# A gated mix of linear and softmax attention on one core: pieces of the output weights rest while the kernel changes halves, and the gate's blocks begin later

## The chip, the cores and the metric

The kernel runs on one core of a Trainium2 chip. The metric is the device time of one execution in microseconds (us), as the median of several runs. Beside the timed runs there is one execution under the hardware profiler; all rows below are from it.

## The reference

```python
def reference(A_x, A_wqkv, A_wo, B_x, B_wqkv, B_wo, gate_w):   # x: 1 x 2048 x 1024, 32 heads of 32
    ...
    x = A_x
    g = _sigmoid((x * gate_w).sum(-1, keepdims=True))
    a = _A_ref(x, A_wqkv, A_wo)      # linear attention: phi(q) (phi(k)^T v) / (phi(q) sum phi(k)), then @ A_wo
    b = _B_ref(x, B_wqkv, B_wo)      # softmax attention over 2048 x 2048 scores per head, then @ B_wo
    return g * a + (1 - g) * b
```

All tensors are float32. The kernel splits each operand into a high part in the reduced format float32r and a low rest, and takes three products (high·high, high·low, low·high) in place of one.

## The kernel before

All instructions of a core's engines are put into their queues in program order, written out by a Python program. Each engine works its queue strictly in order and waits on semaphores for the others. SP issues most transfers, POOL (GpSimd) the rest.

**The first 422 us are a hand-written order.** It has these stages:

- The first half of the tokens is loaded and split, and the first 512 columns of the softmax side's v are computed in eight passes (`v_pass`, one for each block of 128 rows of weights). The weights' splits are stored in DRAM (`wv`).
- `quads(0, ...)` and a last `quad(0, QUADS - 1, ...)`: eight quads, of seven products each, that give the softmax side's q and k for the first half of the tokens by a scheme that needs seven block products in place of eight. A product is 4 × 3 matmuls of 128×512. VectorE (DVE) adds the products (L469 to L486), ScalarE (ACT) and DVE split the results (L294, L295), SP stores them (`qk<-mid`). The same two engines prepare the next quad's weights (`quad_weights`, L428 to L443) from tiles that SP has loaded.
- The products go to six PSUM banks in turn (`turns`, `NQB`): a product has to wait until the adds have read the product six places earlier. The second product of a quad waits so for the adds that end with L478 of the quad before.
- The change of halves: beside the last quad, `change()` loads the stored v weights again (`big<-wv`) and splits the first blocks of the second half of the tokens; then come eight more `v_pass`es, with the splitting of the other blocks (`split_x`, `sides`, `split_sides`), the loading of the first quads' weights, and the copies of v from the banks (`v_out`, L358). The first product of the next quad needs a bank that `v_out` has read.
- `quads(1, ...)` and a last quad: the same for the second half of the tokens.

**The pieces of the output weights** are made beside this. `wo_parts` (L494) is a generator that prepares `b_wo` for the output's seven products: 28 pieces, each with a small copy on ACT (L511) that paces it, a small copy on POOL (L512), a cast and a subtraction on POOL (L513, L514), two stores of 256 KB (L516), on POOL's queue, and, by kind, another POOL subtraction (L524, L531, L537) and a load of 256 KB (L502). It is advanced once at each `next(side, None)` of a quad, seven times a quad, and in the kernel before also twice in each of the eight passes: 49 + 7 + 16 + 49 + 7 = 128 calls. How often a piece comes is set by `PIECE_STEP`:

```python
def wait():
    at[0] += PIECE_STEP
    while next(turn) + 1 < at[0]:
        yield
```

**From 422 us on a planner sets the order.** It keeps a model time for each engine (`T`) and picks the next instruction for PE from four streams: the linear side (`linear`), which begins with the second 512 columns of v ("the last half of v", 16 tiles), the maxima of the scores (L1234, L1239), the heads (L1376, L1379, L1526), and the output. The tiles of the linear side read the split tokens in halves of 256 KB each for high and low (`load_half`; `xh<-xs` and `big<-xs`): three buffers, and a half is loaded into the buffer that has just been used.

**The gate's blocks** (`gate_step`, L553) lie in the last half of v: 32 blocks of the tokens are loaded by SP (`mid<-in_xT`, `zrep<-in_xT`) into four buffers in turn, scaled on ACT (L571), added on POOL (L577) and summed on PE (L585). The first block is issued when PE's model time, counted from the start of the last half of v, is at `GATE_FROM`, and each next one `GATE_STEP` later. A block's load waits on SP's queue until POOL's add has freed its buffer, and all later transfers of SP wait behind it.

Of the kernel before, what the change touches and what calls it, by code (L numbers as in the profile page):

```python
# [38 lines left out]
WARM = 8  # L39
NE = 3  # L40
AHEAD_X = 3
PIECE_STEP = 4.1
GATE_STEP, GATE_FROM = 2.5, 8.0
LATE = 1.0
MANUAL = {ET.PE, ET.DVE, ET.Activation, ET.SP, ET.Pool}
NMID = 13
# [3 lines left out]
def kernel(  # L50
# [34 lines left out]
    def f32r(ap):  # L85
        return ap.bitcast(F32R)
# [62 lines left out]
    def three(ps, stat, mov, kt, late=False, n=None):  # L149

        (sh, sl), (mh_, ml_) = stat, mov
        last = kt == (n or NK) - 1
        yield nc.tensor.matmul(ps, sh, mh_, start=(kt == 0), stop=False)  # L153
        if late:
            yield nc.tensor.matmul(ps, sl, mh_, start=False, stop=False)
        yield nc.tensor.matmul(ps, sh, ml_, start=False, stop=(late and last))  # L156
        if not late:
            yield nc.tensor.matmul(ps, sl, mh_, start=False, stop=last)  # L158
# [8 lines left out]
    def dma(to, of):  # L167

        T["sp"] = max(T["sp"], T["pe"]) + DMA_ISSUE
        nc.sync.dma_start(to, of)  # L170
# [122 lines left out]
    def split(hi, lo, src, eng):  # L293
        nc.scalar.copy(hi, src)  # L294
        eng.tensor_sub(lo, src, f32(hi))  # L295
# [21 lines left out]
    QUADS = 2 * NK // 2  # L317
    assert NK == 8 and NPAIR == 2

    def ring_w(n, p):  # L320

        b, half = RINGW[n % len(RINGW)]
        return big[b][:, (2 * half + p) * C:(2 * half + p + 1) * C]
# [4 lines left out]
    def quad_ring(J, f, s):  # L328
        return v_ring(J, NK) + f * NP + s
# [4 lines left out]
    def xpiece(J, name, p, i):  # L334
        return side_x(J, name, p)[:, i * C:(i + 1) * C]
# [32 lines left out]
    def split_x(raws, J, jj, k, c0=0, c1=C):  # L368
        name = xname(jj, k % 2)
        split(*(xpiece(J, name, p, k // 2)[:, c0:c1] for p in range(2)), raws[jj + 2 * (k % 2)][:, c0:c1], nc.vector)  # L370

    def sides(raws, i):

        r11, r12, r21, r22 = raws
        nc.vector.tensor_sub(r11, r12, r11)
        nc.vector.tensor_sub(r12, r22, r12)
        nc.vector.tensor_sub(r22, r22, r11)
        nc.vector.tensor_sub(t4_raw[i], r21, r22)
# [29 lines left out]
    def quad_cols(f):  # L408
        return f % 2, 2 * (f // 2)
# [37 lines left out]
    def quad(J, f, side):  # L447

        sec, g = quad_cols(f)

        def product(s):
            ps = bank[next(turns) % NQB]
            n = quad_ring(J, f, s)
            for i in range(KH):
                sl = slice(i * P, (i + 1) * P)
                stat = [ring_w(n, p)[:, sl] for p in range(2)]
                for _ in three(ps, stat, [xpiece(J, PRODUCTS[s], p, i) for p in range(2)], i, n=KH):
                    pass
            return ps

        def store(i, jj, src, hi):
            split(f32r(hi), f32r(src), src, nc.vector)
            j = 2 * J + jj
            for p, part in enumerate((hi, src)):
                dma(qk_d[sec][p][g + i][:, j * C:(j + 1) * C], part)

        nc.scalar.copy(P1, product(0))
        next(side, None)
        nc.vector.tensor_add(C11, product(1), P1)  # L469
        store(0, 0, C11, H11)  # L470
        next(side, None)
        p3 = product(2)
        next(side, None)
        p5 = product(3)
        next(side, None)
        nc.vector.tensor_add(U2, product(4), P1)
        nc.vector.tensor_add(W2, p5, U2)
        nc.vector.tensor_add(P1, p3, W2)  # L478
        store(0, 1, P1, H12)
        next(side, None)  # L480
        p7 = product(5)
        nc.vector.tensor_add(W2, p7, W2)
        nc.vector.tensor_add(U2, p7, U2)
        store(1, 1, W2, H22)
        next(side, None)
        nc.vector.tensor_add(U2, product(6), U2)  # L486
        store(1, 0, U2, H21)
        next(side, None)
# [5 lines left out]
    def wo_parts():  # L494

        z0, z1 = halves(zrep)
        hi_w, lo_w = (big[15][:, i * C:(i + 1) * C] for i in (2, 3))
        at, turn, tokens = [1.0], count(), count()

        def load(z, m, i, **add):  # L500
            if i < KH:
                nc.gpsimd.dma_start(z, wo_piece(m, i), **add)  # L502
# [6 lines that stand above are left out]
        def part(m, i, z):  # L509
            n = next(tokens) % (C // DH)  # L510
            nc.scalar.copy(dn[0][:, n:n + 1], eps)  # L511
            nc.gpsimd.tensor_copy(dn[1][:, n:n + 1], dn[0][:, n:n + 1])  # L512
            nc.gpsimd.tensor_copy(hi_w, z)  # L513
            nc.gpsimd.tensor_sub(lo_w, z, f32(hi_w))  # L514
            for p, src in enumerate((hi_w, lo_w)):
                nc.gpsimd.dma_start(wo_d[m][p][:, i * C:(i + 1) * C], f32(src))  # L516

        yield
        load(z1, "W11", 0)
        load(z0, "W21", 0)  # L520
        yield from wait()
        for i in range(KH):
            part("W11", i, z1)
            nc.gpsimd.tensor_sub(z1, z1, z0)  # L524
            load(z0, "W22", i, accum_op=ALU.add)
            yield from wait()
            part("S3", i, z1)
            load(z1, "W11", i)
            yield from wait()
            part("S1", i, z0)  # L530
            nc.gpsimd.tensor_sub(z0, z0, z1)  # L531
            load(z1, "W12", i)
            yield from wait()
            part("S2", i, z0)
            yield from wait()
            part("W12", i, z1)
            nc.gpsimd.tensor_sub(z1, z1, z0)  # L537
            load(z0, "W22", i)
            yield from wait()
            part("S4", i, z1)  # L540
            load(z1, "W11", i + 1)
            yield from wait()
            part("W22", i, z0)
            load(z0, "W21", i + 1)
            yield from wait()

    parts = wo_parts()
# [52 lines left out]
    def beside(*streams):  # L600

        streams = list(streams)
        while True:
            for s in list(streams):
                next(s, None)
            yield
# [30 lines left out]
    def load_wv_again(ks):  # L637
        for k in ks:
            for p in range(2):
                dma(f32(ring_w(v_ring(1, k), p)), wv_d[k][:, p * C:(p + 1) * C])  # L640
# [9 lines left out]
    def load_pair(raws, J, i):  # L650
        for k in (2 * i, 2 * i + 1):
            for jj in range(2):
                load_x(raws, J, jj, k)
# [52 lines left out]
    def change():  # L706

        load_wv_again(range(NK - 2))
        split_x(raw_x1[0], 1, 0, 0)
        yield  # L710
        load_wv_again([NK - 2])
        split_x(raw_x1[0], 1, 1, 0)
        yield
        load_wv_again([NK - 1])
        split_x(raw_x1[0], 1, 0, 1)
        yield
        split_x(raw_x1[0], 1, 1, 1)
        yield
        split_x(raw_x1[1], 1, 0, 2)
        split_x(raw_x1[1], 1, 1, 2)  # L720
        yield
        split_x(raw_x1[1], 1, 0, 3)
        split_x(raw_x1[1], 1, 1, 3)
        yield

    quads(0, lambda: load_pair(raw_x1[0], 1, 0), spill_rest(0), parts)
    load_pair(raw_x1[1], 1, 1)
    quad(0, QUADS - 1, beside(change(), parts))
    for k in range(NK):
        next(parts, None)  # L730
        v_pass(1, k, V_BANKS[1])
        if k == 0:
            sides(raw_x1[0], 0)
            split_sides(raw_x1[0], 1, 0)
            load_pair(raw_x1[2], 1, 2)
        elif k == 1:
            sides(raw_x1[1], 1)
            split_sides(raw_x1[1], 1, 1)
            load_pair(raw_x1[3], 1, 3)
        elif k == 2:  # L740
            for kk in (4, 5):
                for jj in range(2):
                    split_x(raw_x1[2], 1, jj, kk)
            sides(raw_x1[2], 2)
        elif k == 3:
            for kk in (6, 7):
                for jj in range(2):
                    split_x(raw_x1[3], 1, jj, kk)
            sides(raw_x1[3], 3)
            split_sides(raw_x1[2], 1, 2)  # L750
            load_quad(raw_a, 0)
            for _ in spill(1, "X12"):
                pass
        elif k == 4:
            split_sides(raw_x1[3], 1, 3)
            load_quad(raw_b, 1)
        elif k == 5:
            quad_w = quad_weights(raw_a, 1, 0)
            next(quad_w)
            next(quad_w)  # L760
        elif k == 6:
            for _ in quad_w:
                pass
        next(parts, None)
    for t, to in enumerate(v_outs[1]):
        v_out(0, 2 * TPC + t, bank[V_BANKS[1][t]], to)

# [1152 lines left out]
```

## Time and profile before

| What | us |
|---|---|
| median of 3 timed runs | 2843.95 (2843.13 to 2845.47) |
| the profiled execution | 2839.05 |
| its span, first to last instruction | 2837.1 |
| PE busy in the span | 2804.4 |
| DVE, ACT, POOL busy in the span | 2332.1, 1638.2, 2108.2 |

The busy time of PE is modelled from pipelined matmuls: it counts a matmul of 128×512 with 0.39 us while the next one starts 0.23 us later. So the stages are read by their waits and by where matmuls follow one another more slowly, not by the share of busy time. The granted clock of PE is 0.996 over the span.

### The profile page before, as it was taken

Reading aid. Unit: us, or ns where it says so; the run is one execution under the profiler, and the core shown is the slowest. Engines: PE = TensorE matmul, PEld = TensorE weight load, DVE = VectorE, ACT = ScalarE, POOL = GpSimd, SP = SyncE. Lnnn points to the kernel's source line nnn. Section 1 sums busy time; section 2 is a strip of 40 time slices with the busy share of each in tenths; the row PEclk is TensorE's granted clock in tenths of the full one; section 3 lists DMA queues with packets and bytes.
Section 4 is the critical chain, followed back from the end, with each engine's and each line's share of the span. In section 5 each row is a group of like instructions: output and inputs, shape, how many; then the busy total and the mean of one; then the engine's idle time right before and its main releaser. Section 6 shows DMA issues by size and latency. Waiting matters only on the chain.

```text
span 2837.1 us, 47025 instructions
## 1 busy us (share of the span) xinstructions
PE 2804.4 (99%) x15880; PEld 2044.2 (72%) x15880; DVE 2332.1 (82%) x3745; ACT 1638.2 (58%) x3095; POOL 2108.2 (74%) x1150
## 2 busy tenths in 40 slices
PE   9998999999999999999999999999999999999999
PEld 8876887767776677767776677776776667666687
DVE  7886873788888888888888888888888888886688
ACT  5334332466676667666766666666666566665522
POOL 0554324498999998999899998889889988888000
PEclk9999999999999999999999999999999999999999
DMA  8989869633343334333433344455565554544774
GB/s 279 287 272 293 257 217 274 211 91 100 100 131 98 105 105 124 102 95 94 130 101 100 101 128 136 151 167 178 181 201 176 144 155 135 156 121 138 256 236 153
DMA packets 403340, 459.52 MB, mean 162 GB/s; under 512 B 106894, under 2 KB 234894, under 8 KB 401308
## 3 DMA queue, kind: packets, MB, share of 16 engines
q1 hardware_dynamic: 381084, 419.03, 47.1%
q0 software_dynamic: 22016, 37.50, 6.2%
q8 instruction: 126, 2.06, 0.3%
q14 instruction: 114, 0.93, 0.1%
HBM read 314.31 MB, written 127.66 MB: 156 GB/s over the span
## 4 chain that ended last, share of the span: by engine, by line
PE 87%; DMA 4%; DVE 1%; issue 1%; ACT 0%; SPq 0%; POOL 0%; ACTq 0%; DVEq 0%; POOLq 0%
PE bank L1376 17%; PE bank L1234 16%; PE bank L1526 16%; PE bank L153 12%; PE bank L156 12%; PE bank L158 12%; DVE big L295 1%; DMA mid<-in_xT 1%; PE bank L1298 1%; DMA xh<-xs 1%; DMA big<-wv 1%; PE bank L1023 1%; PE bank L912 0%; DMA big<-ra 0%; DMA qk<-mid 0%
## 5 line engine op out<-in xcount | busy, mean ns | idle before, releaser
L1461 POOL TENSOR_TENSOR big<-big,big 128x512 f32<-128x512 f32 (+2 forms) x694 | 1641.7, 2369 | 108.5 <-ACT big L1379 65.8
L1239 DVE TENSOR_REDUCE mx<-bank 128x1 f32<-128x512 f32 x2048 | 1312.3, 681 | 307.3 <-PE bank L1234 303.5
L1379 ACT ACTIVATE big<-bank 128x512 f32<-128x512 f32 x2048 | 1180.0, 602 | 429.8 <-PE bank L1376 363.9
L1376 PE MATMUL bank<-big,big 128*128 128x512 f32 x1888 | 741.6, 394 | 1.8 <-DMA big<-ml 1.1
L1234 PE MATMUL bank<-big,big 128*128 128x512 f32 x1888 | 739.3, 392 | 1.4 <-ACT big L1379 1.4
L153 PE MATMUL bank<-big,big 128*128 128x512 f32 x1576 | 618.6, 393 | 16.8 <-ACT mid L358 9.4
L156 PE MATMUL bank<-big,big 128*128 128x512 f32 x1576 | 615.9, 391 | 0.7 <-DMA big<-wv 0.5
L158 PE MATMUL bank<-big,big 128*128 128x512 f32 x1572 | 614.9, 391 | 1.4 <-DVE big L295 1.4
L1526 PE MATMUL bank<-big,mid 128*32 128x512 f32 x4096 | 454.2, 593 | 0.0
L1376 PEld LDWEIGHTS bank<-big,big 128*128 128x128 f32 x1888 | 354.0, 188 | 126.6 <-issue 48.6
L1234 PEld LDWEIGHTS bank<-big,big 128*128 128x128 f32 x1888 | 354.6, 188 | 75.3 <-ACT big L1379 2.8
L153 PEld LDWEIGHTS bank<-big,big 128*128 128x128 f32 x1576 | 297.0, 188 | 86.7 <-ACT mid L358 9.8
L158 PEld LDWEIGHTS bank<-big,big 128*128 128x128 f32 x1572 | 295.9, 188 | 65.9 <-DVE big L295 3.2
L156 PEld LDWEIGHTS bank<-big,big 128*128 128x128 f32 x1576 | 296.9, 188 | 63.0 <-DMA big<-wv 0.9
L1526 PEld LDWEIGHTS bank<-big,mid 128*32 128x32 f32 x4096 | 143.9, 110 | 264.1 <-issue 263.8
L1477 DVE TENSOR_TENSOR bank<-bank,big 128x512 f32<-128x512 f32 x364 | 251.4, 691 | 5.6 <-ACT big L1379 3.3
L294 ACT CAST big<-mid 128x512 fp32r<-128x512 f32 (+1 forms) x157 | 92.8, 618 | 118.6 <-DVE mid L1645 66.0
L295 DVE TENSOR_TENSOR big<-mid,big 128x512 fp32r<-128x512 f32 (+1 forms) x157 | 121.1, 787 | 44.5 <-ACT big L294 44.3
L1457 POOL TENSOR_TENSOR big<-big,big 128x1536 f32<-128x1536 f32 (+1 forms) x31 | 123.3, 3978 | 41.0 <-ACT big L1379 41.0
L153 PE MATMUL bank<-big,xh 128*128 128x512 f32 x376 | 148.1, 394 | 5.3 <-DMA xh<-xs 5.3
L158 PE MATMUL bank<-big,xh 128*128 128x512 f32 x376 | 147.8, 393 | 0.0
L156 PE MATMUL bank<-big,xh 128*128 128x512 f32 x376 | 147.7, 393 | 0.0
(163 smaller groups left out, 2131.8 us busy)
## 6 DMA issues: line engine op xcount, KB each, us to landing
big<-xs SPq DMA_DIRECT2D x288, 256.0 KB
big<-qk SPq DMA_DIRECT2D x690, 64.0 KB
xh<-xs SPq DMA_DIRECT2D x144, 256.0 KB
qk<-mid SPq DMA_DIRECT2D x128, 256.0 KB
big<-oA SPq DMA_DIRECT2D x84, 256.0 KB
xs<-big SPq DMA_DIRECT2D x64, 256.0 KB
oA<-mid SPq DMA_DIRECT2D x64, 256.0 KB
big<-big POOLq DMA_DIRECT2D x50, 256.0 KB, 5.6
```

The costliest lines, as they stand in the source:

```text
L153: yield nc.tensor.matmul(ps, sh, mh_, start=(kt == 0), stop=False)
L156: yield nc.tensor.matmul(ps, sh, ml_, start=False, stop=(late and last))
L158: yield nc.tensor.matmul(ps, sl, mh_, start=False, stop=last)
L295: eng.tensor_sub(lo, src, f32(hi))
L1234: nc.tensor.matmul(bank[b], q[:, t % TPC * P:(t % TPC + 1) * P], k[:, j * C:(j + 1) * C], start=True, stop=True)
L1239: nc.vector.tensor_reduce(m[:, t, j:j + 1], bank[b], AX.X, ALU.max)
L1376: nc.tensor.matmul(bank[b], k[:, t * P:(t + 1) * P], q_cols(h, j), start=True, stop=True)
L1379: nc.scalar.activation(pr_t[i][:, j * C:(j + 1) * C], bank[b], AF.Exp, scale=SCALE)
L1457: nc.gpsimd.tensor_add(lacc[:, :qp], pr(0)[:, :qp], pr(1)[:, :qp])
L1461: nc.gpsimd.tensor_add(lacc[:, sl], lacc[:, sl], pr(t)[:, sl])
L1477: nc.vector.tensor_add(lacc[:, qp:] if t == NT - 1 else l_b[:, :n], l_b[:, :n], src)
L1526: nc.tensor.matmul(av_b[j * DH:(j + 1) * DH, :], v[:, t, :], pr(t)[:, j * C:(j + 1) * C], start=(t == 0), stop=(t == NT - 1))
```

## The change

`PIECE_STEP` goes from 4.1 to 3.4. The generator of the pieces is no longer advanced in the last quad of the first half and in the eight passes behind it: the calls are 49 + 49 + 7 = 105. `GATE_FROM` goes from 8 to 20 us and `GATE_STEP` from 2.5 to 2.3 us. No instruction is added or taken away; what moves is where the pieces and the gate's blocks stand in the queues, and what the planner makes of it.

```diff
-PIECE_STEP = 4.1
-GATE_STEP, GATE_FROM = 2.5, 8.0
+PIECE_STEP = 3.4
+GATE_STEP, GATE_FROM = 2.3, 20.0
...
     load_pair(raw_x1[1], 1, 1)
-    quad(0, QUADS - 1, beside(change(), parts))
+    quad(0, QUADS - 1, change())
     for k in range(NK):
-        next(parts, None)
         v_pass(1, k, V_BANKS[1])
...
         elif k == 6:
             for _ in quad_w:
                 pass
-        next(parts, None)
     for t, to in enumerate(v_outs[1]):
```

## The prediction

> **What bounds the kernel now.** I read the waits of PE over the whole run first, because the share of busy time says 99% everywhere. In each row stand: who waited, for whom, us in total, times, the longest.
>
> ```profile
> PE bank L153 <- ACT mid L358: 9.4, 1, 9.4
> PE bank L153 <- DMA xh<-xs: 5.3, 2, 4.6
> PE bank L153 <- DVE mid L478: 4.0, 4, 2.2
> ```
>
> PE waits for little, and nearly all of it lies before 570 us, in the part that the change touches. The timeline of PE places the three longest waits:
>
> ```profile
> 150.69 0.47 PE L153 MATMUL bank<-big,big 128*128 128x512 f32 x1 [2.22 <-DVE mid L478]
> 154.50 0.63 PE L158 MATMUL bank<-big,big 128*128 128x512 f32 x1
> 266.44 0.79 PE L153 MATMUL bank<-big,big 128*128 128x512 f32 x1 [9.39 <-ACT mid L358]
> 456.70 0.79 PE L153 MATMUL bank<-big,xh 128*128 128x512 f32 x1 [4.58 <-DMA xh<-xs]
> ```
>
> One wait lies in the first half's quads, one at the end of the eight passes, one in the last half of v. Behind each the matmuls take 0.63 us instead of 0.39 for 3 to 5 us: the clock has dropped, and each matmul starts 0.2 us later. That costs 2 to 3 us more after the long ones (10 and 14 matmuls) and 1.6 after the 2.22 (8). Busy time by stage (us, busy of PE, PEld, DVE, ACT, POOL, granted clock, DMA share, GB/s) shows who is short of time where:
>
> ```profile
> 70.00:198.00 128.00, 123.97 (x535) 100.77 (x534) 110.84 (x138) 43.24 (x89) 68.08 (x88) 0.99 0.89 279
> 198.00:275.00 77.00, 63.98 (x267) 50.90 (x266) 53.37 (x67) 28.63 (x58) 40.46 (x51) 0.93 0.90 288
> 276.00:335.00 59.00, 58.82 (x259) 47.90 (x257) 51.81 (x69) 20.91 (x43) 27.20 (x35) 1.00 0.83 264
> 340.00:400.00 60.00, 60.00 (x266) 49.71 (x265) 48.31 (x76) 22.57 (x41) 0.00 (x0) 1.00 0.75 237
> 422.00:462.00 40.00, 35.41 (x146) 28.56 (x146) 2.75 (x5) 8.98 (x15) 23.60 (x36) 0.92 0.90 260
> ```
>
> In the quads (first, third, fourth row) DVE is busy four fifths of the time and more; in the change of halves (second row) PE loses 13 us and the transfers are at 0.90; in the fifth row the transfers are at 0.90 and PE loses 4.6.
>
> **Where the pieces go.** The pacing copies on ACT, by stage, count the pieces:
>
> ```profile
> 55.00:198.00 143.00, 2.61 (x14) 0.99 0.86 271
> 198.00:275.00 77.00, 1.49 (x8) 0.93 0.90 288
> 275.00:340.00 65.00, 1.12 (x6) 1.00 0.85 267
> ```
>
> The code gives the same. The call in which a piece comes uses up two numbers of the turn, so a piece comes every 3.1 calls at a step of 4.1: calls 7, 10, ... 47 (14 pieces) in the first 49, 50 to 72 (8) in the change, 75 to 90 (6) in the second quads. With 3.4 one comes every 2.4 calls: 6, 8, ... 49 (19 pieces) in the first 49, none in the change, and 51 to 71 of 105 (9) in the second quads. So 8 pieces leave the change, 5 go into the first quads, 3 into the second.
>
> **What a piece costs in the quads.** The groups of DVE from 55 to 198 us, and then from 340 to 402 us, where no piece runs (count, busy us, mean ns of one, idle before):
>
> ```profile
> L295 DVE TENSOR_TENSOR big<-mid,big 128x512 fp32r<-128x512 f32 x38 | 37.9, 1014 | 10.1 <-ACT big L294 10.1
> L295 DVE TENSOR_TENSOR mid<-mid,mid 128x512 fp32r<-128x512 f32 x27 | 20.7, 767 | 15.5 <-ACT mid L294 14.7
> L295 DVE TENSOR_TENSOR big<-xh,big 128x512 fp32r<-128x512 f32 x9 | 9.9, 1095 | 0.0
> L430 DVE TENSOR_TENSOR xh<-xh 128x512 f32<-128x512 f32 x3 | 5.8, 1932 | 0.1
> ```
>
> ```profile
> L295 DVE TENSOR_TENSOR big<-mid,big 128x512 fp32r<-128x512 f32 x16 | 10.8, 685 | 1.1 <-ACT big L294 1.1
> L295 DVE TENSOR_TENSOR mid<-mid,mid 128x512 fp32r<-128x512 f32 x14 | 9.7, 692 | 8.4 <-ACT mid L294 8.0
> ```
>
> The same instruction is longer where pieces run: 38 × 0.329 + 27 × 0.075 + 9 × 0.410 + 3 × 1.25 (the last two against 685 ns) = 22 us for 14 pieces, 1.6 us a piece. The timelines of POOL and of DVE (start, us) show how:
>
> ```profile
> 94.20 0.61 POOL L513 CAST big<-zrep 128x512 fp32r<-128x512 f32 x1
> 94.90 1.29 POOL L514 TENSOR_TENSOR big<-zrep,big 128x512 fp32r<-128x512 f32 x1
> 97.26 1.29 POOL L531 TENSOR_TENSOR zrep<-zrep 128x512 f32<-128x512 f32 x1
> ```
>
> ```profile
> 95.55 1.19 DVE L295 TENSOR_TENSOR mid<-mid,mid 128x512 fp32r<-128x512 f32 x1 [0.73 <-ACT mid L294]
> 96.67 2.45 DVE L295 TENSOR_TENSOR big<-mid,big 128x512 fp32r<-128x512 f32 x1
> ```
>
> A subtraction of DVE ends only when POOL's has ended; these two lose 0.50 and 1.76 us, 2.3 in all. And DVE's own cadence sets the pace of the first quads:
>
> ```profile
> 108.96 0.69 DVE L478 TENSOR_TENSOR mid<-bank,mid 128x512 f32<-128x512 f32 x1
> 191.04 0.69 DVE L478 TENSOR_TENSOR mid<-bank,mid 128x512 f32<-128x512 f32 x1
> ```
>
> ```profile
> 346.39 0.69 DVE L478 TENSOR_TENSOR mid<-bank,mid 128x512 f32<-128x512 f32 x1
> 363.08 0.69 DVE L478 TENSOR_TENSOR mid<-bank,mid 128x512 f32<-128x512 f32 x1
> ```
>
> The first two are four quads apart, 20.5 us each; the last two one quad, 16.7 us, without pieces. PE needs 84 matmuls, 84 × 0.227 = 19.05 us (60 us hold 266 recorded matmuls with no gap, 0.226 each). So with pieces DVE is the slower one and PE follows it.
>
> **The sum, against the profiled execution of 2839.05 (span 2837.1 and 1.95 around it).** The median of the runs is 4.9 above it; I carry the difference over to the median.
>
> First quads: up to the seventh L478, which releases PE, 17 pieces stand (calls up to 46) instead of 13. 4 × 1.6 = **+6.5 us**. Nothing hides it, since DVE is the slower one; the lower bound is +3, if POOL falls behind and two of the four slip, the upper 4 × 2.3 = +9. The Trainium skill, SBUF — State Buffer, "Who interferes with whom", speaks against this move: a DVE instruction with two SBUF inputs and a GpSimd instruction that reads SBUF exclude each other for whole instructions, so that the later one fully waits. The trace agrees in kind; taken as a full wait behind each of POOL's three instructions (0.61 + 1.29 + 1.29) the page would make it 4 × 3.2 = 13, an estimate, while the trace has DVE lose 2.3 there.
>
> Change of halves: the chain of waits leads to the 9.39.
>
> ```profile
> 203.43 8.81 DMA big<-wv
> 219.03 7.31 DMA qk<-mid
> 264.93 0.49 ACT mid L358
> ```
>
> From 203 to 226 us it is transfers: 16 loads of v's weights, behind them on SP the quad's stores, and DVE's L378 waits for one of them to free its buffer. From 226 on it is DVE and ACT with loads between. POOL's queue took about a quarter of the transfers:
>
> ```profile
> q0 software_dynamic: 1500, 4.73, 24.4%
> woS<-big POOLq DMA_DIRECT2D x8, 256.0 KB, 4.3
> ```
>
> (130 to 190 us: 24.4% of the 60 us for its 7 pieces, 2.1 us a piece.) Without it the 23 us become about 17; DVE gets back 8 × 1.6 us in the stage, about half of it on this chain; the loads between come 1 to 2 us sooner (my estimate, a quarter of some 6 us each). That is 6 + 6 + 1.5 = 13.5 against the wait of 9.4, so the wait goes and its slow clock (2 us) with it. What is late next is v's weights, about 1 us, since SP's order is unchanged. PE loses 13 + 2 us here now; I leave 3.5: **-11.5 us**, between -7 (pieces trail in, half the wait stays) and -14.
>
> Second quads: three pieces more, and DVE there runs with no room (PE's gaps in the third row are 0.2 us). 3 × 1.6 = 4.8. ACT's copies L358, now from 264.93 on, will come while the banks fill, so that DVE begins these quads less far behind, by my estimate 2.3 us: **+2.5 us**, from 0 to +5.
>
> Last half of v: the chain before the 4.58.
>
> ```profile
> 435.57 10.63 DMA mid<-in_xT
> 449.76 1.36 SPq L170
> 451.23 5.43 DMA xh<-xs
> ```
>
> A gate block takes 10.6 us to land, POOL's add is late, and SP, which holds the gate's next load until the add has freed the buffer, issues the half of tokens only at 451.23. `GATE_FROM` = 20 puts the first blocks 12 us later, behind the rush of POOL's first loads. The new step moves nearly nothing: the planner counts 0.2275 us a matmul, and 2.5 and 2.3 are both reached at the 11th. Moved past on SP are stores of v and halves of tokens; both get earlier. I take the wait and its slow clock (4.6 + 2.8) away and leave 2 for blocks and halves that now start together: **-5.5 us**, between -7.4 and 0.
>
> Beginning of the heads: the gate's last blocks now lie beside the loads of the next weights.
>
> ```profile
> 546.07 0.50 PE L1234 MATMUL bank<-big,big 128*128 128x512 f32 x1 [1.45 <-ACT big L1379]
> ```
>
> ACT was late here by those loads; five blocks more in front on SP: **+1 us**, from 0 to +4. A gain is excluded while the loads stay last. The remaining 2280 us are the planner's order with other starting times; the same instructions, 0 ± 2.
>
> 6.5 - 11.5 + 2.5 - 5.5 + 1 = -7.0: 2832 for the profiled execution, **2837.0 us** for the median. A clock that drops after 2.2 us of idleness is already in the rows; the Trainium skill, TensorE: Matmul & The Clock Gate, Part 1, puts the idle window at about 3.4 us, and by it the shorter waits would cost no slow clock. The trace disagrees (0.63 at 154.50), and the measurement decides.
>
> **The rivals.** *Crowded quads (slower).* The eight quads with three pieces (six and two) lose more than DVE's 1.6 us a piece: the share of POOL's transfers rises from 24 to 32%, that of all from 0.89 to 0.96, and a store of `qk` lands after 7.3 us, as at 219.03, not after 5, so that the next quad's first copy waits for its buffer. At 2.3 us more in each, 8 × 2.3 = 18, the sum is +11: 2855. It decides from 0.9 us a quad on, where the gain of 7 is gone. For it: 0.89 is high. Against: a quad stretched by DVE spreads the transfers too. Chance 0.24.
>
> *The change keeps its wait (no change).* The chain there is order on SP and DVE, not traffic: only DVE's half, 5 us, comes back and is eaten by the waits between. -5 in place of -11.5: -0.5, 2843.5. Chance 0.06.
>
> *The gate's new place is no better.* Blocks meet halves of tokens at 445 us instead of POOL's loads: 0 in place of -5.5, and +2 at the heads: +0.5, 2844.5. Chance 0.05.
>
> *Pieces cost the quads nothing more.* POOL cannot hold the step, since a store lands after 4.3 us and the next cast waits for it; the extra pieces spread over the passes, where DVE has room: +3 - 14 + 0 - 7.4 + 0 = -18: 2825.5. Chance 0.12.
>
> *Each piece holds DVE for all of POOL's reading (no change).* 3.2 us a piece instead of 1.6: 4 × 3.2 = 13 in the first quads, 3 × 3.2 - 2.3 = 7 in the second, +4.5 with the other terms: 2848. This is the rule of the skill's page above, taken in full. Against it: of 3.2 us the trace has DVE lose 2.3 at the worst and 1.6 on average. Chance 0.03.
>
> **How the numbers follow.** The forecast has 0.50; its own range is 2829 to 2842, from the bounds of the terms. A measurement of this kernel can tell 0.2% from no change, 5.7 us: faster is below 2838.3, slower above 2849.6. Two thirds of the forecast and the fourth rival are faster: 0.34 + 0.12 = 0.46. A third of the forecast, the second, third and fifth rivals are the same: 0.16 + 0.14 = 0.30. Slower 0.24. The range 2827 to 2853 leaves out the far half of the slower rival and part of the fourth.
>
> **What would show it.** Right: 19, 0 and 9 copies L511 by stage; L478 of the first quads 21.5 us apart with a wait of 2 to 3 us in each quad; no wait of PE for L358 above 2 us; none for `xh<-xs` above 2. Wrong: a distance of L478 above 23 us, the 9.4 still there, or waits of PE in the second quads of over 5 us together.

## The result, and the profile after

The changed kernel takes **2832.33 us** (median of 5 runs, 2829.2 to 2836.14) against 2843.95 of the kernel before (5 runs, 2841.47 to 2845.47): a ratio of 0.9959, 95% interval 0.9944 to 0.9973. The span of the profiled execution falls by 6.8 us, from 2837.1 to 2830.3.

First the waits of PE in the kernel after (who waited, for whom, us in total, times, the longest):

```profile
PE bank L153 <- DVE mid L478: 6.4, 5, 2.5
PE bank L153 <- DMA big<-xs: 3.2, 1, 3.2
PE bank L153 <- DMA big<-wv: 3.0, 1, 3.0
PE bank L153 <- DMA xh<-xs: 1.2, 2, 0.9
PE bank L153 <- ACT mid L358: 0.9, 1, 0.9
```

The two longest waits of before are nearly gone (L358 from 9.4 to 0.9, `xh<-xs` from 5.3 to 1.2), but two that were not there have come, for `big<-wv` and for `big<-xs`. The timeline of PE says where:

```profile
190.38 0.77 PE L153 MATMUL bank<-big,big 128*128 128x512 f32 x1 [2.53 <-DVE mid L478]
211.47 0.76 PE L153 MATMUL bank<-big,big 128*128 128x512 f32 x1 [2.96 <-DMA big<-wv]
259.39 0.50 PE L153 MATMUL bank<-big,big 128*128 128x512 f32 x1 [0.88 <-ACT mid L358]
526.82 0.50 PE L153 MATMUL bank<-big,big 128*128 128x512 f32 x1 [3.24 <-DMA big<-xs]
```

`big<-wv` is the reload of v's weights in the change of halves, `big<-xs` a half of tokens near the end of the last half of v. Now the stages (us, then busy us of PE, PEld, DVE, ACT, POOL, then granted clock, DMA share, GB/s), for the same stretches as before:

```profile
70.00:198.00 128.00, 123.50 (x536) 100.88 (x535) 112.21 (x138) 43.27 (x93) 81.56 (x111) 0.99 0.95 299
198.00:275.00 77.00, 72.66 (x308) 58.95 (x307) 52.45 (x78) 32.42 (x59) 9.27 (x13) 0.96 0.81 259
422.00:462.00 40.00, 39.10 (x169) 30.96 (x168) 7.89 (x12) 8.75 (x14) 17.27 (x26) 1.00 0.95 280
```

In the first quads POOL has 13.5 us more work and the transfers rise to 0.95, yet PE executes as many matmuls as before (536 against 535). In the change of halves it executes 41 more. The pieces, counted by the copies L511 on ACT (55 to 198, 198 to 275, 275 to 340 us), stand nearly where they should, but the second row is not empty: of its two copies one, at 199.9 us, belongs to the first quads' last piece, the other, at 272.5, to the second quads:

```profile
55.00:198.00 143.00, 3.37 (x18) 0.99 0.92 290
198.00:275.00 77.00, 0.37 (x2) 0.96 0.81 259
275.00:340.00 65.00, 1.50 (x8) 1.00 0.87 277
```

The rest of the text works with five stretches, cut at instructions that every kernel has: the start of the seventh L478 (the end of the first quads, as the prediction counts them), the first matmul of the second quads, the last L478, the first exponential of the heads, the last one.

| us, from the traces | start of 7th L478 | to 2nd quads | to last L478 | to first exponential | to last one |
|---|---|---|---|---|---|
| before | 191.0 | 75.4 | 151.8 | 127.2 | 2122.5 |
| after | 189.5 | 69.8 | 153.6 | 124.3 | 2123.8 |
| difference | -1.5 | -5.6 | +1.8 | -2.8 | +1.3 |

### The profile page after: what moved, and what is told of

The parts are those of the page before. It is cut to its first block, busy times and chain, and to the rows that moved or that the text cites. A ratio compares the mean times of both kernels' runs of the same rounds, so it can differ in the third digit from the quotient of the medians.

```text
span 2830.3 us, 47031 instructions
## 1 busy us (share of the span) xinstructions
PE 2803.5 (99%) x15880; PEld 2043.9 (72%) x15880; DVE 2331.1 (82%) x3745; ACT 1638.6 (58%) x3095; POOL 2103.2 (74%) x1150
## 4 chain that ended last, share of the span: by engine, by line
PE 85%; DMA 1%; issue 0%; DVE 0%; SPq 0%; ACT 0%; ACTq 0%; DVEq 0%
PE bank L1374 17%; PE bank L1232 16%; PE bank L1524 16%; PE bank L153 11%; PE bank L158 11%; PE bank L156 11%; PE bank L1296 1%; PE bank L1021 1%; PE bank L910 0%; DMA big<-ra 0%; DMA xh<-xs 0%; PE bank L1288 0%; SPq L170 0%; DMA big<-xs 0%; DMA extra<-in_a_wqkv 0%
## 5 line engine op out<-in xcount | busy, mean ns | idle before, releaser
L1232 PEld LDWEIGHTS bank<-big,big 128*128 128x128 f32 x1888 | 354.6, 188 | 75.4 <-ACT big L1377 3.1
```

The source lines that it names most:

```text
L1232: nc.tensor.matmul(bank[b], q[:, t % TPC * P:(t % TPC + 1) * P], k[:, j * C:(j + 1) * C], start=True, stop=True)
```

## The experiments

### The parts of the change

All of the pieces' part, with the old gate:

```diff
 PIECE_STEP = 3.4                          # as after, rest included
-GATE_STEP, GATE_FROM = 2.3, 20.0
+GATE_STEP, GATE_FROM = 2.5, 8.0
```

> The pieces' part of the change alone (step 3.4, no pieces in the change of halves); the gate as before. By the milestones of the two traces the pieces moved the start of the last half of v by -5.3 us (first quads -1.5, change of halves -7.6, second quads +4). Theory A (both parts gain, the pieces more): about -5 us against before, the wait for L358 under 1 us, the wait of 4.6 for xh<-xs still there. Theory B (the gate's place is the whole gain): 0 us, since what the change of halves gives, the quads take.

Measured: 2834.32 against 2842.35, 0.997 (0.9959 to 0.998). The change of halves is that of the changed kernel (69.8 us), with a wait of 3.8 for `big<-wv`. The first theory is borne out in its signs: PE still waits 5.1 us for `xh<-xs`, and waits 2.0 for L358, not under 1 as expected. The seventh L478 starts at 192.8 us here and at 189.5 in the changed kernel, with identical instructions up to there: a stretch of one trace is good to about 3 us.

The gate alone: the kernel before with `GATE_STEP, GATE_FROM = 2.3, 20.0`.

> The gate's part alone (from 20 us, step 2.3); the pieces as before. Theory A: about -2 to -4 us against before: the wait of 4.6 for xh<-xs near 460 us goes, a wait of about 3 for big<-xs comes near 525 us; the 9.4 us wait for L358 stays. Theory B: -7 to -11 us, the whole change. Theory C (the gate only matters after a change of the pieces): 0 us.

Measured: 2840.63 against 2842.35, 0.9994 (0.9986 to 1.0003): not told apart from no change. The waits move as the first theory had it (for `xh<-xs` the longest is 1.9, for `big<-xs` 1.6, for L358 11.0), but its 2 to 4 us are not resolved. The last half of v gains 2.4 us (124.8 in place of 127.2), and the stretch behind the first exponential loses 1.8 (2124.4).

The rest alone: the change, with the old step and the old gate.

```diff
-PIECE_STEP = 3.4
-GATE_STEP, GATE_FROM = 2.3, 20.0
+PIECE_STEP = 4.1
+GATE_STEP, GATE_FROM = 2.5, 8.0
```

> The pieces rest in the change of halves but keep the step of 4.1, so 14 pieces come in the first quads, none in the change, 14 in the second quads; the gate as before. Theory A (DVE pays 1.4 to 1.8 us for each piece in a quad, as POOL's reading holds it): first quads as before, the 9.4 wait gone, and the second quads, now with 2.3 pieces in each of six, cost about 4 us more: -5 us in all. Theory D (the transfers of the pieces and not POOL's reading are what costs): the second quads cost 0, -9 us in all.

Measured: 2834.07, 0.9972 (0.996 to 0.9983). Resting alone brings as much as all of the pieces' part. The change of halves takes 62.9 us here, 12.5 less than before and 6.9 less than with the shorter step; the second quads, with 14 pieces, take 158.8, 7 more. So the pieces cost the second quads more than either theory said, and the change of halves gives more back.

The step alone: the kernel before with `PIECE_STEP = 3.4`, so that nine pieces lie in the change of halves.

> The shorter step alone, with the pieces still in the change of halves: 19 pieces in the first quads, 9 in the change, none in the second quads; the gate as before. Theory A: first quads -1 to +2 us, the wait for L358 at least the 9.4 of before since the change holds one piece more, the second quads -0.5: 0 +- 3 us against before. Theory E (the shorter step is what gains, since the pieces are over sooner): -5 us.

Measured: 2846.84, 1.0008 (0.9999 to 1.0017). The wait in the change nearly doubles:

```profile
PE bank L153 <- ACT mid L358: 17.5, 1, 17.5
```

The change takes 86.4 us. So the shorter step brings nothing that these runs can tell, without the rest or with it.

The rest with the new gate: the changed kernel with `PIECE_STEP = 4.1`.

> The changed kernel with the old step of 4.1: pieces rest in the change, 14 in the first and 14 in the second quads, the gate from 20 us. If the parts add up: rest alone -8.3, gate alone -1.7: -10 us against before. If the gate gains more once the pieces rest (changed kernel against pieces alone: -3.5): -12 us, no slower than the changed kernel. The second quads cost about 6 us more than before, as with rest alone, and the wait for v's weights is under 1 us.

Measured: 2834.08 against 2842.01, 0.997 (0.9961 to 0.9979). The change takes 62.8 us again. The gate brings 4.6 us in the last half of v against the kernel with the rest alone and gives 1.4 back behind the first exponential; the ratios of the two are the same within their intervals. By the medians the gain is 8 us, short of both sums that were expected (10 and 12).

### What of a piece hurts in the change: its transfers or POOL's reading

Both kernels are the kernel before with one half of the eight pieces of the change taken out. In the first the cast and subtractions of pieces 15 to 22 are left out; loads and stores stay.

```diff
-            nc.gpsimd.tensor_copy(hi_w, z)
-            nc.gpsimd.tensor_sub(lo_w, z, f32(hi_w))
+            n_part[0] += 1
+            if not 15 <= n_part[0] <= 22:
+                nc.gpsimd.tensor_copy(hi_w, z)
+                nc.gpsimd.tensor_sub(lo_w, z, f32(hi_w))
...
-            nc.gpsimd.tensor_sub(z1, z1, z0)
+            sub(z1, z0)          # the same bounds; so the other two
```

> The kernel before, but the 8 pieces in the change of halves (pieces 15 to 22) keep their loads and stores and leave out POOL's cast and subtractions (so their values are not the reference's). It tells the two costs of these pieces apart: traffic, and DVE held by POOL's reading. With all of it the wait for L358 is 9.4 to 11 us; with none of it (rest alone) it was 1.2 and the ninth L478 came 11.8 us sooner. The prediction's step (6 us of the chain is traffic, 6 is DVE): half, a wait of 3 to 5 and the ninth L478 5 to 7 us sooner. Theory of traffic alone: as before, a wait of 9 or more. Theory of DVE alone: a wait of 1 to 2, 11 us sooner.

In the second the loads of these pieces are left out and their stores come after the last piece; the reading stays.

```diff
-            if i < KH:
+            if i < KH and not 14 <= n_part[0] <= 22:
...
+            if n_part[0] < 15 or n_part[0] > 22:      # the stores, as before
...
+            else:
+                owed.extend((m, i, p, src) for p, src in enumerate((hi_w, lo_w)))
...                                                    # after the last piece: one store a call
```

> The kernel before, but the 8 pieces in the change of halves keep POOL's cast and subtractions and leave out their loads, and their stores are issued later, in the second quads (so their values are not the reference's). The prediction's step: a wait for L358 of 2 to 4 us, the ninth L478 5 to 7 us sooner than before. Theory of traffic alone: a wait of 1 to 2, 11 us sooner. Theory of DVE alone: as before, 9 or more.

Measured: 2839.75 and 2837.74 (one run each) beside 2842.01 of before. The waits of PE, of the kernel with transfers only and then of that with reading only:

```profile
PE bank L153 <- ACT mid L358: 4.1, 1, 4.1
PE bank L153 <- DMA big<-wv: 3.7, 1, 3.7
```

```profile
PE bank L153 <- ACT mid L358: 6.7, 1, 6.7
```

The change takes 72.3 us without the reading (3.1 less) and 69.7 without the transfers (5.7 less); without both, in the kernel with the rest alone, 12.5 less. The ninth L478, by which the expectation measured, comes in the kernel before, with transfers only, with reading only and with the rest alone at

```profile
289.15 0.69 DVE L478 TENSOR_TENSOR mid<-bank,mid 128x512 f32<-128x512 f32 x1
289.26 0.69 DVE L478 TENSOR_TENSOR mid<-bank,mid 128x512 f32<-128x512 f32 x1
280.95 0.69 DVE L478 TENSOR_TENSOR mid<-bank,mid 128x512 f32<-128x512 f32 x1
277.36 0.69 DVE L478 TENSOR_TENSOR mid<-bank,mid 128x512 f32<-128x512 f32 x1
```

By then nothing is left of what the first kernel won: taking out the reading alone brings the next quads nothing, taking out the transfers alone 8.2 us, both 11.8. So "half and half" fails in both kernels (5 to 7 us were expected in each), and neither of the one-sided theories fits all four waits and times. The transfers are the greater part, and the reading shows once they are gone; each size rests on one run. With transfers alone the matmuls wait for v's weights as they do in the changed kernel.

### What makes DVE the slower one in the first quads

The kernel before, with cast and subtractions of pieces 2 to 14 left out as above, and all transfers kept:

> The kernel before, with POOL's cast and its subtractions left out in pieces 2 to 14, those of the first quads; their loads, stores and pacing copies stay. Left out of the computation: the splitting of these pieces, so the softmax side's output is not the reference's. One theory says that DVE, held by POOL's reading, is what makes DVE the slower one in the first quads. Then the distance of L478 falls from 20.5 us to PE's own 84 matmuls, about 19.1 us, PE's waits for L478 before 191 us go (4.0 us in all now), and the seventh L478, at 191.0 us in the kernel before, ends 6 to 8 us sooner, at 183 to 185. The rival says that it is the transfers of the pieces that make DVE's operands late: these stay, so the distances stay at 20 to 20.5 us and the seventh L478 within 2 us of 191.

Measured: 2827.74, one run, beside 2843.21. The timeline of DVE:

```profile
121.83 0.69 DVE L478 TENSOR_TENSOR mid<-bank,mid 128x512 f32<-128x512 f32 x1
140.88 0.69 DVE L478 TENSOR_TENSOR mid<-bank,mid 128x512 f32<-128x512 f32 x1
159.91 0.69 DVE L478 TENSOR_TENSOR mid<-bank,mid 128x512 f32<-128x512 f32 x1
178.95 0.69 DVE L478 TENSOR_TENSOR mid<-bank,mid 128x512 f32<-128x512 f32 x1
```

19.04 us apart, PE's own 84 × 0.2267, and no wait for L478 is left in these quads. It is POOL's cast and subtractions, not the traffic of the pieces; their reading and their writing are left out together here. The size was expected too small: 12.1 us in place of 6 to 8, since DVE, which begins these quads behind, first makes up ground (the third quad takes 16.7 us).

### Why the changed kernel gets only half in the change

The three pieces of the seventh quad are held back until after the change:

```diff
-PIECE_STEP = 3.4
+PIECE_CALLS = [6, 8, 11, 13, 15, 18, 20, 23, 25, 27, 30, 32, 35, 37, 39, 42,
+               51, 54, 56, 59, 61, 64, 66, 68, 71, 73, 76, 78]
...
         def wait():
-            at[0] += PIECE_STEP
-            while next(turn) + 1 < at[0]:
+            while when:                       # when = deque(PIECE_CALLS)
                 yield
+                now[0] += 1
+                if now[0] >= when[0]:
+                    when.popleft()
+                    return
```

> The changed kernel with its closer pieces, but only 16 of them before the change of halves (calls 6, 8, 11 to 42): the three of the seventh quad (calls 44, 47, 49) are held back to calls 51, 54 and 56, and the nine others follow up to call 78. One theory says that the change of halves gives only half of what resting gives because pieces that POOL could not hold at this pace slip into the last quad, where their reads hold DVE and their stores lie beside the reloads of v's weights. Then, with none left to slip, the stretch from the seventh L478 to the first matmul of the second quads falls from 69.9 us to the 62.9 us of the kernels with the old pace, the wait for big<-wv of 3 us goes, the second quads take 2 to 4 us more (12 pieces in place of 9), and the time is 2826 to 2829. The rival says that the loss comes with the closer pace as such, by what has piled up on the queues before: the stretch stays at 68 us or more, the wait for big<-wv at 3 us, and the time is 2832 to 2835.

Measured: 2829.84 against 2841.31, 0.9958 (0.9944 to 0.9971). The change takes 62.0 us, the second quads 157.9. The first matmul of the second quads, and the reloads on SP's queue (duration min/median/max in ns, first and last start), here and then in the changed kernel:

```profile
253.03 0.50 PE L153 MATMUL bank<-big,big 128*128 128x512 f32 x1 [0.53 <-ACT mid L358]
L170 SPq DMA_DIRECT2D big<-wv x16: 319/320/917, 201.6 to 214.0; - x16
```

```profile
L170 SPq DMA_DIRECT2D big<-wv x16: 319/320/2086, 204.5 to 219.8; - x16
```

Without the three pieces the reloads begin 2.9 us sooner, take 3 us less, and nobody waits for them. DVE is done sooner too: the last quad's L478 comes 14.1 us after the seventh, not 20.3 as in the changed kernel, where DVE's subtractions beside POOL's three pieces take up to 2.46 us, not 0.69. How the loss divides between the two was not tested. Of the 7.8 us won in the change the second quads take back 4.3, and the time lies just above the 2826 to 2829 that were expected. Against the changed kernel the ratios overlap; what is shown is the cause of the lost half, not a faster kernel.

### Pieces at chosen places

A piece's price on DVE differs with its kind and its place in the quad: in the traces from 0 to 3.3 us. The next three kernels write the calls out by hand, so that pieces of each kind come where such pieces had cost little, and none is called in the change.

```diff
+PIECE_CALLS = [10, 13, 17, 20, 24, 26, 29, 32, 36, 39, 43, 46, 50, 54,
+               59, 62, 66, 69, 73, 75, 78, 81, 85, 88, 92, 95, 99, 103]   # gate 2.3, 20.0
```

> As the kernel with rest, a step of 4.1 and the late gate, but the pieces come at chosen calls, two in each of 14 quads: by the traces so far a piece costs DVE 0 to 0.6 us or 1.5 to 3 us, by its kind and by the place in the quad where it comes, since POOL's reading holds only DVE's instructions with two operands in SBUF and falls beside others (adds from PSUM, waits for ACT) for nothing. Pieces with a POOL subtraction behind are put at the third or fourth call of a quad, the others at the first, fourth, fifth or sixth. Theory P (price by place): about 1.05 us a piece, 2.1 a quad, less than the 2.3 that DVE has to spare: waits for L478 under 4 us in all, first quads 4 us or more sooner than before, second quads at most +2, -17 us against before. Theory A (a fixed price of 1.4 to 1.8): 2 pieces a quad as with the step of 4.1, -10 to -12 us.

Measured: 2825.58 against 2842.01, 0.9945 (0.9932 to 0.9957). The waits for L478 are 2.4 us in all, the seventh L478 starts at 183.5, the change takes 63.8: the theory of a price by place holds, except that the second quads take 4.3 us more than before (156.1), not at most 2. But PE waits for a half of tokens although the gate is late:

```profile
439.81 0.79 PE L153 MATMUL bank<-big,xh 128*128 128x512 f32 x1 [5.45 <-DMA xh<-xs]
```

The last pieces, at calls 99 and 103, stand in front of and among POOL's loads `big<-qk`, which begin at 399.9 us; POOL's casts for the two start at 396.4 and 413.7. So the last ones come sooner, and the others move a little too:

```diff
+PIECE_CALLS = [8, 11, 15, 18, 22, 25, 28, 32, 35, 39, 42, 46, 49, 50,
+               53, 56, 60, 63, 67, 70, 74, 77, 81, 84, 88, 91, 95, 97]    # gate 2.3, 20.0
```

> As the kernel with chosen calls, and the gate from 20 us at steps of 2.3, but the pieces of the second quads stand closer together, so that the last comes at call 97 in place of 103, before the first loads of the linear side on POOL's queue. One theory says that the wait for xh<-xs of 5.4 us near 440 us in the kernel with chosen calls comes from these loads being pushed back by the last pieces. Then it is below 1.5 us here, and the time is 4 to 5 us lower than there, some 2821 us (20 to 22 below the kernel before). The rival says that the wait belongs to the stage itself: the wait stays at 4 to 5 us and the time at 2825 to 2826, or the closer pieces cost the second quads 3 us or more and it is 2828.

Measured: **2821.19** (2819.82 to 2822.8) against 2843.21, 0.9926 (0.9914 to 0.9939). The wait is 1.82 in place of 5.45 (below 1.5 was expected), and the time 4.4 lower, as the first theory had it; by which way the last pieces had made that half of tokens late was not traced:

```profile
436.15 0.50 PE L153 MATMUL bank<-big,xh 128*128 128x512 f32 x1 [1.82 <-DMA xh<-xs]
517.36 0.50 PE L153 MATMUL bank<-big,big 128*128 128x512 f32 x1 [2.86 <-DMA big<-xs]
```

This kernel has the lowest median of all. The same calls with the gate of before (2.5, 8.0):

> The same chosen calls, the last at 97, with the gate of the kernel before (from 8 us, steps of 2.5). One theory says that the gate's later blocks bring what the prediction says, 4.5 us net: then this is 4 to 5 us slower than the same calls with the later gate, with a wait for xh<-xs of 4 us or more. The second says that the later gate brings 1 to 2 us, as it did alone and beside the prediction's other half, since a wait for big<-xs of 2 to 3 us near 525 us takes the place of that one: then this is 1 to 2 us slower. The third says nothing is left of it: within 0.7 us.

Measured: 2823.09 (2820.59 to 2826.79), 0.9933 (0.9919 to 0.9946): 1.9 slower by the medians, with intervals that overlap. One wait of PE in the last half of v, and none for `big<-xs` above 0.3:

```profile
443.26 0.79 PE L153 MATMUL bank<-big,xh 128*128 128x512 f32 x1 [8.05 <-DMA xh<-xs]
```

## Why the prediction was right in its sum, and where its steps failed

The forecast was 2837.0 in a range of 2827 to 2853; the measured 2832.33 lies in it, and the spans of the profiled executions differ by 6.8 us where the steps gave 7.0 (the medians by 11.6). The near agreement is luck: two of the steps were wrong by 8 and by 6 us (the second by 4, counted alike), more than a trace's 3, a third by 2.7, and the errors cancelled. Two of its figures don't come out of its own terms, with no weight for the result: the last rival's sum is about +4, not +4.5, and the bounds of the terms, added up, give 2825.6 to 2855, not 2829 to 2842.

**First quads: +6.5 predicted, -1.5 in this trace, about 0 over all traces. This step failed.** It took 1.6 us from DVE's mean loss per piece before and charged it to each further piece. Four traces have the closer pieces up to the seventh L478 (189.5, 192.8, 190.9 and 191.0 us), six the old step (191.0 to 192.0). The groups of DVE from 55 to 198 us, after:

```profile
L295 DVE TENSOR_TENSOR big<-mid,big 128x512 fp32r<-128x512 f32 x38 | 37.8, 1012 | 9.6 <-ACT big L294 9.6
L295 DVE TENSOR_TENSOR mid<-mid,mid 128x512 fp32r<-128x512 f32 x27 | 23.9, 884 | 15.5 <-ACT mid L294 14.6
L295 DVE TENSOR_TENSOR big<-xh,big 128x512 fp32r<-128x512 f32 x9 | 7.2, 804 | 0.0
L295 DVE TENSOR_TENSOR big<-extra,big 128x512 fp32r<-128x512 f32 x6 | 7.0, 1162 | 0.0
L432 DVE TENSOR_TENSOR mid<-mid,mid 128x512 f32<-128x512 f32 x4 | 5.6, 1403 | 0.0
L430 DVE TENSOR_TENSOR xh<-xh 128x512 f32<-128x512 f32 x3 | 3.1, 1048 | 0.1
```

By the prediction's own reckoning (692 ns for the second row, 685 for the others): 38 × 0.327 + 27 × 0.192 + 9 × 0.119 + 6 × 0.477 + 4 × 0.718 + 3 × 0.363 = 25.5 us for 18 pieces, 1.4 a piece, where it had 22 for 14. The stretch that counts, from the first to the seventh L478, shows it more plainly: what DVE's instructions with two operands in SBUF took above 0.69 us adds up to 23.1 us before, with 13 casts of POOL, and to 22.1 after, with 16; over the ten traces it is 21.7 to 24.2 with 13 and 22.1 to 23.1 with 16. Three more pieces cost nothing there. That DVE is held by POOL was right (with POOL's cast and subtractions taken out, PE set the pace); what is not fixed is the price. In every trace each of these instructions that took over 0.74 us, between 70 and 420 us, overlapped a cast or a subtraction of POOL, so a piece costs what it meets. At chosen places 12 casts cost 11.2 us in the same stretch. Why the closer pieces met less was not followed piece by piece. The adds from PSUM are not touched: the eight L478 up to 210 us, after, have min, median and max of

```profile
L478 DVE TENSOR_TENSOR mid<-bank,mid x8: 691/691/692, 68.2 to 209.9; 128x512 f32<-128x512 f32 x8
```

The Trainium skill, SBUF — State Buffer, "Who interferes with whom", says that a DVE instruction with at most one SBUF input does not contend with GpSimd. The trace agrees, 691 to 692 ns in every one, and the prediction cited only the half of that section that speaks of two inputs. Its lower bound, +3, counted two slipped pieces; one of the 17 had slipped.

So the L478 were not 21.5 us apart, as foretold, but 19.9 ((189.55 − 109.90) / 4), by these rows (20.2 to 20.5 in the three other traces with these pieces):

```profile
109.90 0.69 DVE L478 TENSOR_TENSOR mid<-bank,mid 128x512 f32<-128x512 f32 x1
189.55 0.69 DVE L478 TENSOR_TENSOR mid<-bank,mid 128x512 f32<-128x512 f32 x1
```

**Change of halves: -11.5 predicted, -5.6 measured (-7.6 counted alike).** The prediction counted 2 us of slow clock here that the table has in the second quads. The reason held. With the old step the rest alone gave -12.5, in two kernels (-14.5 counted alike, a little beyond the upper bound of 14). The failed step is that pieces which stand before the change were taken to run before it. POOL's timeline after:

```profile
183.97 0.77 POOL L513 CAST big<-zrep 128x512 fp32r<-128x512 f32 x1 [2.81 <-DMA woW<-big]
190.07 0.61 POOL L513 CAST big<-zrep 128x512 fp32r<-128x512 f32 x1 [1.82 <-DMA woS<-big]
202.57 0.61 POOL L513 CAST big<-zrep 128x512 fp32r<-128x512 f32 x1 [1.79 <-DMA woS<-big]
204.95 1.10 POOL L516 DMA_DIRECT2D woW<-big  x2
```

The last three casts start from 190 to 203 us, in the last quad, with stores issued until 206, where v's weights are to be reloaded. Two things put them there. ACT's copies for them stand at 182.8, 191.4 and 199.9, so the last two come behind the seventh L478 by their place in the order alone. And POOL doesn't hold the step: three of its last four casts wait until stores of a piece before have landed, and the last three start 7.3, 4.0 and 2.7 us behind their copies. Holding these three pieces back removed the wait of 2.96 for `big<-wv` and brought the change to 62.0 us. The prediction allowed for this ("pieces trail in", -7) and chose a middle value.

Its split of the 11.5 into six for the transfers, six for DVE and 1.5 for the loads between isn't borne out as a sum: taking out the transfers alone brought 5.7 in this stretch, the reading alone 3.1, which was gone by the ninth L478, and both 12.5.

**Second quads: +2.5 predicted, +1.8 measured (+3.8 counted alike).** Within what a trace can say. The kernels with 14 and 12 pieces there (158 to 159 and 157.9 us) show the same trade.

**Last half of v: -5.5 predicted, -2.8 measured; beginning of the heads and the rest: +1 predicted, +1.3.** The wait for `xh<-xs` went, as foretold, but a new one for `big<-xs` came at 526.82, inside the same stage, with a slow clock behind it (matmuls of 0.63 us from 528.10 on); the 2 us left "for blocks and halves that now start together" were too little. Every kernel with the later gate has this wait (2 to 3.3 us in all), those with the earlier gate have 0 to 1.4. In the four pairs that differ by the gate alone, the stage gains 1.9 to 4.6 us, and the stretch behind changes by -0.4 to +1.8. By the medians the gate is worth 0 to 2 us, in no pair resolved.

**The rivals.** *Crowded quads* did not come: at a DMA share of 0.95 no instruction of ACT or DVE waits for a store of `qk` in the quads; only DVE's L378, in the change, still does, 5.2 us in place of 7.1. *Pieces cost the quads nothing more* was right for the first quads, by another reason than its own: the slipping that it counted on does no good, since late pieces run in the change. *The change keeps its wait* falls with the row of 0.88; *the gate's new place is no better* and the forecast lie about equally far from the measured gate: by the rival the gate costs 2 us or more, by the forecast it gives 4.5, by the medians 0 to 2. *Each piece holds DVE for all of POOL's reading* falls with the 1.4 us a piece.

## What to carry to other kernels

The mean price of background work is no price for one more piece of it: ask which instruction of the slower engine each piece meets, and place it by hand where that engine reads what the other doesn't hold up. Here the same 28 pieces at chosen calls, with none called in the change of halves, took 22 us off the kernel before together with the later gate and 20 with the old one, where the change took 12. And when work is kept out of a stage, look at what stands just before it and whether its queue is on time, for work that stands at the end of the stage before, or that is late, runs in the stage after all.

## What was not expected of the hardware

- One piece has POOL read SBUF for up to 3.2 us when nothing holds it (0.61 + 1.29 + 1.29), and cost DVE between 0 and 3.3 us by its place. Six quads with 13 casts lost 23.1 us (what DVE's instructions with two operands in SBUF took above 0.69, added up), the same six with 16 casts 22.1.
- Transfers and reading of POOL together cost the change of halves 12.5 us, but taking out one of them alone brought 5.7 or 3.1: part of the gain stays hidden behind the other.
- Whether a wait of PE of less than 3 us costs a slow clock isn't told by its length; between 60 and 2700 us, all longer ones did. In the kernel with the rest and the new gate a wait of 2.91 us that ended at 151.68 left the granted clock at 1.00, and one of 1.81 us that ended at 172.78 was followed by eight matmuls of about 0.63 us, at a mean clock of 0.83. So a term like the prediction's 1.6 us of slow clock behind the wait of 2.22 can come or stay away from one trace to the next. The two stretches:

```profile
148.00:157.00 9.00, 6.09 (x28) 4.75 (x27) 7.85 (x13) 2.42 (x5) 1.34 (x3) 1.00 0.96 330
170.00:180.00 10.00, 8.19 (x30) 6.27 (x29) 8.34 (x13) 4.41 (x9) 4.37 (x8) 0.83 0.62 214
```

- How late POOL's stores of 256 KB land does not follow POOL's share of the transfers: the median of `woS<-big` from 130 to 190 us is 4.3 us at a share of 24.4% (before) and 4.7 at 34.2% (after), but 5.9 at 23.5% with the chosen calls and the old gate.
